# Converting float64 weights in word operations: carrying the sign through ScalarE's scaling instead of a second VectorE operation

## The chip, the cores and the metric

The kernel runs on one NeuronCore of one Trainium2 chip. The metric is the time of one execution on the device, in microseconds (us). The time of before is the median of three runs.

## The reference

The inputs are float64; the output is float32 of 4352 x 512. Three layers follow each other: an attention between x (8 batches, 8 heads, 512 rows, width 64) and a state of 32 rows per batch and head, and two gated layers.

```python
scores = scale * np.matmul(x, state.transpose(0, 1, 3, 2))      # softmax, then xread = a @ state
scores2 = scale * np.matmul(state, x.transpose(0, 1, 3, 2))     # softmax, then sread = a2 @ x
x = np.concatenate([xread, sread], axis=2)                      # reshaped to 4352 x 512
x = (x @ w1) * (x @ w2) @ w3 @ w_out                            # moe: 512 -> 1024 -> 512
x = (x @ w_a) * (x @ w_b) @ w_out                               # moe2: 512 -> 1536 -> 512
```

What matters here is that all seven weight matrices arrive as float64 and must be made float32 on the chip before TensorE can use them.

## The kernel before, in words

**Tiles and buffers.** SBUF is handed out as 47 numbered units of 128 x 1024 words, PSUM as 8 banks of 128 x 512. A unit that is taken again carries the wait for its former use with it, on whatever engine writes it first, a load's queue included.

**The conversion.** A load brings 128 x 512 float64 numbers (512 KB) into one unit as pairs of 32-bit words. Such a load is called a piece. `Convert` (from L154) makes float32 of a piece in four operations:

- `take` (L165): two ScalarE activations. The first (L167) reads the upper words as float32 and multiplies them by 2^-112, in place. Seen as a float32, the upper word of a float64 has the upper 8 of the 11 exponent bits as its exponent, so the scaling subtracts 112 there, which is 896 = 1023 - 127 in the exponent of the float64. The second (L170) scales the lower words by 2^-29 into integers.
- `shift` (L172): a VectorE `tensor_scalar` (L176) moves the upper words left by 3 bits; exponent and mantissa are then where float32 has them, and the sign is shifted out. A VectorE `scalar_tensor_tensor` (L179) takes the sign bit of the unshifted word by a bitwise and, and puts it into the result by a bitwise or.
- `add` (L183): a GpSimd integer addition (L185) puts in the bits of the lower word, and the unit of the load becomes free.

There are 92 pieces: 40 at the start (20 names of two pieces in `EARLY`, L24), 16 for the first gated layer's state path (`sw`), and 36 for the second layer (`ab`: twelve column blocks of two pieces, each with one piece of the output matrix).

**Stages.** At the start, the pieces of `w_out` (`wo`) are converted and split into a high and a low float32r part (`woh` by ScalarE L297, `wol` by VectorE or GpSimd L303); those of `w3` are converted, transposed by TensorE (L347), split (`w3h`, `w3l`), and multiplied by `w_out` in `weight_product` (L361), which needs all of `wo`; `ws` is the result. The pieces of `w1` and `w2` (`wk`) are multiplied by the state (L318), copied to SBUF (`sg`, L330 and L332), stored to DRAM per batch (L336, `p_d`) on SP's queue, and loaded again (L593, `pr`), split into `ph` (L136) and `pl` (L142), and multiplied by the attention weights (`f`, L1054). In the middle, batch after batch goes through the first layer (L1054, L1113) while the attention of the next batch and the `sw` and `ab` conversions are laced in. From some 600 us on, the second layer runs (L1500, L1512), TensorE's long part; it uses no conversion after 700 us.

**What sets the order.** The program is written out by hand, one queue per engine. At the start, `run_jobs` (L646) is a list scheduler: each `Job` (L603) names its engine, a price in us, its predecessors and the units and banks that it needs; the job that can start first by these prices is written next. `convert_jobs` (L678) makes the jobs of a piece: ScalarE 1.3, VectorE 1.45 (L691), GpSimd 1.3. Jobs that may go to either of two engines (`wol`, `sg`) are put where they would end first by the prices. In the middle, `Intake` (L898) holds the steps of `sw` and `ab` blocks, each with its prices (`V=1.8, G=2.4` for two pieces, L997; `V=0.9, G=1.2` for one, L1008); a step is written once the time counted for its engines has come near. These prices are numbers in the program that orders the instructions; the chip doesn't see them.

Of the kernel before, what the change touches and what calls it, by code (L numbers as in the profile page):

```python
# [9 lines left out]
F32 = mybir.dt.float32  # L10
# [4 lines left out]
AF = mybir.ActivationFunctionType  # L15
ALU = mybir.AluOpType
# [43 lines left out]
def attention_moe_moe2(  # L60
# [17 lines left out]
    nc = tc.nc  # L78
# [38 lines left out]
    def unit(name, dt=F32):  # L117
        assert name not in held, name
        first = min(range(len(vacant)), key=lambda i: vacant[i][0])
        held[name] = vacant.pop(first)[1]  # L120
        return up.tile([P, 1024], dt, tag=f"u{held[name]}", name=name)

    def free(*names, at=None):
        for name in names:
            vacant.append((at or until[0] or now[0], held.pop(name)))
# [23 lines left out]
    def load64(name, src):  # L149
        t = unit(name, U32)  # L150
        nc.sync.dma_start(out=t if len(src.shape) == 2 else flat(t, src.shape[2]), in_=src)
        return name, t

    class Convert:  # L154
# [10 lines left out]
        def take(self, i):  # L165
            c, d = self.words(i)
            nc.scalar.activation(  # L167
                out=c.bitcast(F32), in_=c.bitcast(F32), func=AF.Copy, scale=2.0**-112
            )
            nc.scalar.activation(out=d.bitcast(I32), in_=d, func=AF.Copy, scale=2.0**-29)  # L170

        def shift(self, i):  # L172
            if self.out is None:
                self.out = unit(self.name)[:, : self.n]
            c, out = self.words(i)[0], self.out[:, i * 512 : (i + 1) * 512].bitcast(U32)
            nc.vector.tensor_scalar(  # L176
                out=out, in0=c, scalar1=3, scalar2=None, op0=ALU.logical_shift_left
            )
            nc.vector.scalar_tensor_tensor(  # L179
                out=out, in0=c, scalar=0x80000000, in1=out, op0=ALU.bitwise_and, op1=ALU.bitwise_or  # L180
            )

        def add(self, i):  # L183
# [487 lines left out]
    def load_job(time, go, need, lag=1.0):  # L671
        j = Job("D", time, go, behind=loads[-1:], need=need, keep=KEEP if len(loads) < KEEP_UNTIL else 1, prio=len(loads), lag=lag)
        loads.append(j)
        return j

    conv = {}

    def convert_jobs(name):  # L678

        adds = []  # L680
        conv[name] = Convert(name, [None, None])
        for i, v in enumerate(parts[name]):

            def load(i=i, v=v):
                conv[name].raws[i] = load64(f"{name}r{i}", v)

            l = load_job(1.7, load, 1)
            if len(loads) == 1:
                state_jobs()
            t = Job("A", 1.3, lambda i=i: conv[name].take(i), after=[l], prio=2)  # L690
            s = Job("V", 1.45, lambda i=i: conv[name].shift(i), after=[t] + adds, need=1 - i, prio=2)  # L691
            adds = adds + [Job("G", 1.3, lambda i=i: conv[name].add(i), after=[s], prio=2)]
        return adds

# [121 lines left out]
    for name in EARLY:  # L816
# [3 lines left out]
        elif name[:2] == "wo":  # L820
            i = int(name[2])
# [3 lines left out]
        elif name[:2] == "w3":  # L825
            i = int(name[3])
            adds = convert_jobs(name)
            lows, trs = [], []
            for k in range(2):
# [4 lines left out]
                    after=list(adds),  # L834
                    prio=0,
# [6 lines left out]
                    after=[tr] + lows,  # L842
                    need=2 - 2 * k,
                    prio=1,
# [6 lines left out]
                        after=[h],  # L851
                        prio=1,
# [20 lines left out]
        else:  # L873
            b = int(name[1])
            done = []
            for g in range(2):
                l = load_job(3.5, lambda b=b, g=g: load_x_half(b, g), 1, 2.0)
                t = Job("P", 1.8, lambda b=b, g=g: attn[b].x_transpose(g), after=[l], need=1, prio=1, banks=("ps", 2))
# [19 lines left out]
    class Intake:  # L898
# [27 lines left out]
        def stages(self, f, raws):  # L926

            o = {}
            name = f"{self.name}{f}"
            eng = "GV"[f % 2]  # L930

            def take(i):
                if i == 0:
                    o["c"] = Convert(name, raws[:2])
                o["c"].take(i)

            def take_third():
                o["t"] = Convert(f"{name}t", raws[2:])
                o["t"].take(0)

            def split_columns():
                hi, lo = unit(f"{name}h", F32R), unit(f"{name}l", F32R)
                split(hi, lo, o["c"].out, {"G": nc.gpsimd, "V": nc.vector}[eng])
                free(name)
                self.cols[f] = [v.rearrange("p (w k c) -> p w k c", k=4, w=2) for v in (hi, lo)]

            def halves(t):
                return t.rearrange("p (b c) -> p b c", b=4)

            def sums():  # L950
                a21, a22, a11, a12 = (halves(o["c"].out)[:, i] for i in range(4))
                o["s"] = unit(f"{name}s")
                s1, s2, s3, s4 = (halves(o["s"])[:, i] for i in range(4))
                e = {"G": nc.gpsimd, "V": nc.vector}[eng]
                for out, x, y, op in (
                    (s1, a21, a22, ALU.add),
                    (s3, a11, a21, ALU.subtract),
                    (s2, s1, a11, ALU.subtract),
                    (s4, a12, s2, ALU.subtract),
                ):  # L960
                    e.tensor_tensor(out=out, in0=x, in1=y, op=op)

            def split_part(i):
                src, part = ((o["c"].out, name), (o["s"], f"{name}s"))[i]
                hi, lo = (unit(f"w0_{f}_{2 * i + j}", F32R) for j in range(2))
                split(hi, lo, src, {"G": nc.gpsimd, "V": nc.vector}["VG"["GV".index(eng)]])
                free(part)
                o["p", i] = hi, lo

            def store_part(i):  # L970
                for j, t in enumerate(o["p", i]):
                    nc.sync.dma_start(out=w_d[f][:, 2 * i + j].bitcast(F32), in_=t.bitcast(F32))
                if f in AB_AT:
                    free(*(f"w0_{f}_{2 * i + j}" for j in range(2)), at=until[0] + 2.5)
                else:
                    w_t.setdefault((0, f), []).extend(
                        t.rearrange("p (b k c) -> p b k c", b=4, k=2) for t in o["p", i]
                    )
                self.cols[f] = i == 1

            def split_third():
                z = o["z"] = flat(unit(f"z{f}", F32R), DM)
                split(z[:, 0, :], z[:, 1, :], o["t"].out)
                free(f"{name}t")

            def store_third():
                nc.sync.dma_start(out=z_d[f].bitcast(F32), in_=o["z"].bitcast(F32))
                if f in AB_AT:
                    free(f"z{f}", at=until[0] + 2.5)
                else:  # L990
                    z_t[f] = o["z"]
                self.rows[f] = True

            out = [
                (0, dict(A=1.1), lambda: take(0)),
                (0, dict(A=1.1), lambda: take(1)),
                (1, dict(V=1.8, G=2.4), lambda: o["c"].make()),  # L997
            ]
            if self.third is None:
                out.append((2, {"A": 1.1, eng: {"G": 2.4, "V": 1.1}[eng]}, split_columns))  # L1000
            else:
                other = "VG"["GV".index(eng)]
                work = {"A": 1.1, other: {"G": 2.4, "V": 1.1}[other]}
                out += [
                    (0, dict(A=1.1), take_third),
                    (1, {eng: {"G": 2.6, "V": 1.4}[eng]}, sums),
                    (2, work, lambda: split_part(0)),
                    (1, dict(V=0.9, G=1.2), lambda: o["t"].make()),  # L1008
                    (0, dict(D=3.0), lambda: store_part(0)),
                    (2, work, lambda: split_part(1)),  # L1010
                    (1, dict(A=0.6, V=0.6), split_third),
                    (0, dict(D=3.0), lambda: store_part(1)),
                    (0, dict(D=1.5), store_third),
                ]
            return deque(out)
# [301 lines left out]
    for b, qs in ((0, range(4)), (1, range(3))):  # L1317
        for q in qs:
# [4 lines left out]
                after=stores[q // 2] + ([last] if last else []),  # L1323
                need=1,
                prio=1 + 20 * b,
# [7 lines left out]
    for f in range(NF1):  # L1333
# [4 lines left out]
            after=[ready[0, f // 2], attended[0][0]],  # L1338
# [12 lines left out]
    for p in range(NP):  # L1351
        for nh in range(2):
            products = []
            moves = {0: [], 1: []}
            for i in range(2):
# [4 lines left out]
                    after=[last],  # L1360
                    need=2 - 2 * i,
                    keep=LATE_KEEP,
                    prio=LATE_PRIO,
# [10 lines left out]
            for r in range(2):  # L1374
# [4 lines left out]
                    after=moves[r],  # L1379
                    prio=len(loads) + STORE_BEHIND,  # L1380
# [4 lines left out]
    for j in range(4):  # L1385
        o = Job("P", 5.5, lambda j=j: first_output(j), after=lows + w_done + moves[-2:-1], prio=8, banks=("ps", 1))
# [399 lines left out]
```

## Time and profile before

| what | us |
|---|---|
| median of the three runs | 1377.65 |
| lowest and highest of them | 1375.01, 1380.78 |
| span of the profiled execution (first to last instruction) | 1376.4 |
| TensorE (PE) busy | 1308.8 |
| VectorE (DVE) busy | 697.6 |
| ScalarE (ACT) busy | 550.8 |
| GpSimd (POOL) busy | 445.2 |

The profiled execution's own time is recorded only as its span; what lies around the span is taken as the 1.25 us by which the median is longer. In the profile, PE is TensorE's matmuls, PEld its weight loads; a name with a q behind it is that engine's queue. A window row gives, for each engine, busy us and, in brackets, the number of instructions, then the granted TensorE clock as a share of full speed, the DMA share and GB/s. A row of waits gives who waited for whom, the total, the times, and the longest.

### The profile page before, as it was taken

To read this page: it belongs to the slowest core of one execution; us is meant where nothing else is said; L and a number is where in the kernel's file an instruction comes from. 1 tells how busy PE (TensorE), PEld (TensorE's weight loads), DVE (VectorE), ACT (ScalarE), POOL (GpSimd) and SP (SyncE) were. 2 spreads that over 40 slices of the span, in tenths; PEclk is the share of its full clock that TensorE was granted. 3 is DMA by queue.
4 is the path that set the end of the run, shared out by engine and by line. 5 is a ranking of instruction groups with operands and counts; after the bars stand their busy time and mean duration, and the time that the engine had idled before them with its cause. 6 is when DMAs were issued, how large, how long until landed. Compare 5 with 4: busy or idle time off the path is not lost.

```text
span 1376.4 us, 17480 instructions
## 1 busy us (share of the span) xinstructions
PE 1308.8 (95%) x6596; PEld 1056.0 (77%) x6596; DVE 697.6 (51%) x879; ACT 550.8 (40%) x955; POOL 445.2 (32%) x353
## 2 busy tenths in 40 slices
PE   2888999999999998999999999999999999999998
PEld 1655678788777777988888888888888888888877
DVE  7997405666768767566652442232632224532241
ACT  6676534556555565454431322211412223311230
POOL 4543402554465465445530152111311112310010
PEclk6899999999999999999999999999999999999999
DMA  9675758364655651467554436443464443744401
GB/s 321 219 222 181 216 160 242 133 210 167 225 184 174 224 168 63 139 229 291 185 194 171 169 122 230 153 145 116 152 233 165 153 138 122 262 158 145 140 0 62
DMA packets 120661, 240.24 MB, mean 175 GB/s; under 512 B 44672, under 2 KB 65152, under 8 KB 120576
## 3 DMA queue, kind: packets, MB, share of 16 engines
q1 hardware_dynamic: 116000, 222.86, 48.8%
q0 software_dynamic: 4576, 16.26, 3.1%
q8 instruction: 52, 0.85, 0.2%
q14 instruction: 33, 0.27, 0.1%
HBM read 173.54 MB, written 65.54 MB: 174 GB/s over the span
## 4 chain that ended last, share of the span: by engine, by line
PE 70%; DVE 5%; ACT 2%; issue 2%; DMA 1%; POOL 1%; SPq 0%; DVEq 0%; POOLq 0%; ACTq 0%
PE o L1512 19%; PE r L1500 18%; PE v L1500 9%; PE x2p L1113 6%; PE q L1500 5%; PE bp L1054 3%; PE ap L1054 3%; PE abs L1555 2%; PE os L1584 1%; DVE sw L179 1%; PE x2s L1113 1%; DMA w_d<-w 1%; DMA z<-z_d 1%; PE as L1054 1%; PE bs L1054 1%
## 5 line engine op out<-in xcount | busy, mean ns | idle before, releaser
L1512 PE MATMUL o<-z,h 128*128 128x512 f32 x1152 | 276.8, 389 | 2.1 <-ACT h L136 1.3
L1512 PEld LDWEIGHTS o<-z,h 128*128 128x128 f32 x1152 | 216.0, 188 | 48.2 <-ACT h L136 1.7
L1675 POOL TENSOR_TENSOR hb<-e,e 128x512 f32<-128x512 f32 x48 | 62.8, 1309 | 448.5 <-DVE e L1525 448.5
L136 ACT CAST h<-e 128x512 fp32r<-128x512 f32 x48 | 29.8, 620 | 369.7 <-DVE e L1678 355.6
L1113 PE MATMUL x2p<-hp,ws 128*128 128x512 f32 x672 | 161.9, 390 | 0.0
L1113 PEld LDWEIGHTS x2p<-hp,ws 128*128 128x128 f32 x672 | 125.7, 188 | 26.3
L1525 DVE TENSOR_TENSOR e<-e,q 128x512 f32<-128x512 f32 x48 | 33.0, 687 | 193.9 <-PE q L1500 193.9
L142 POOL TENSOR_TENSOR pl<-pr,ph 128x512 fp32r<-128x512 f32 x64 | 85.6, 1357 | 114.7 <-ACT ph L136 99.5
L1078 DVE TENSOR_TENSOR hfp<-asbp,bp 128x512 f32<-128x512 f32 x56 | 38.2, 682 | 77.7 <-PE bp L1054 76.0
L1525 DVE TENSOR_TENSOR e<-e,v 128x512 f32<-128x512 f32 x48 | 32.9, 686 | 80.4 <-PE v L1500 80.4
L1500 PE MATMUL r<-xT4h,w 128*128 128x512 f32 x192 | 67.3, 391 | 2.6 <-DVE e L1525 2.6
L136 ACT CAST hp<-hfp 128x512 fp32r<-128x512 f32 x56 | 34.7, 619 | 81.4 <-DVE hfp L1078 78.9
L142 DVE TENSOR_TENSOR hp<-hfp,hp 128x512 fp32r<-128x512 f32 x56 | 46.8, 836 | 40.0 <-ACT hp L136 38.6
L1500 PE MATMUL r<-xT2h,w 128*128 128x512 f32 x192 | 67.1, 390 | 0.0
L1500 PE MATMUL r<-xB11h,w 128*128 128x512 f32 x192 | 66.9, 389 | 0.0
L1500 PE MATMUL v<-xT1h,w 128*128 128x512 f32 x192 | 66.9, 389 | 0.0
L1500 PE MATMUL q<-xB21h,w 128*128 128x512 f32 x192 | 66.9, 389 | 0.0
L1500 PE MATMUL r<-xT3h,w 128*128 128x512 f32 x192 | 66.9, 389 | 0.0
L1500 PE MATMUL v<-xB22h,w 128*128 128x512 f32 x192 | 66.9, 389 | 0.0
L1054 PE MATMUL bp<-ah,ph 128*128 128x512 f32 x112 | 48.7, 435 | 5.0 <-DVE hfs L1078 3.1
L142 DVE TENSOR_TENSOR h<-e,h 128x512 fp32r<-128x512 f32 x48 | 35.1, 732 | 33.4 <-ACT h L136 33.4
L1072 ACT COPY asbp<-ap 128x512 f32<-128x512 f32 x56 | 32.8, 585 | 46.2 <-PE ap L1054 46.1
(505 smaller groups left out, 2928.1 us busy)
## 6 DMA issues: line engine op xcount, KB each, us to landing
w<-w_d SPq DMA_DIRECT2D x168, 512.0 KB, 5.2
w_d<-w SPq DMA_DIRECT2D x48, 512.0 KB, 2.7
p_d<-sg SPq DMA_DIRECT2D x128, 128.0 KB, 2.5
pr<-p_d SPq DMA_DIRECT2D x32, 512.0 KB, 5.4
x<-in_x_dram SPq DMA_DIRECT2D x64, 128.0 KB, 3.7
sw<-in_moe_w_dram SPq DMA_DIRECT2D x16, 512.0 KB, 5.1
xB<-x_d SPq DMA_DIRECT2D x16, 512.0 KB, 5.1
x_d<-x2sp POOLq DMA_DIRECT2D x14, 512.0 KB, 5.7
```

The source lines that it names most:

```text
L136: nc.scalar.copy(hi, src)
L142: (eng or nc.vector).tensor_tensor(out=lo[:, i], in0=src[:, i], in1=hi[:, i].bitcast(F32), op=ALU.subtract)
L179: nc.vector.scalar_tensor_tensor(out=out, in0=c, scalar=0x80000000, in1=out, op0=ALU.bitwise_and, op1=ALU.bitwise_or)
L1054: nc.tensor.matmul(dst[:, :n], lhsT=l[m], rhs=r[q], start=i == 0 and j == 0, stop=i == k - 1 and j == 2,)
L1072: nc.scalar.copy(a_sb[:, :n], pa[:, :n])
L1078: nc.vector.tensor_tensor(out=hf[:, :n], in0=a_sb[:, :n], in1=pb[:, :n], op=ALU.mult)
L1113: nc.tensor.matmul(acc[j], lhsT=w_s[f][:, m, j * P : (j + 1) * P], rhs=h[:, q, :n], start=per == 1 and f == 0 and i == 0, stop=f == NF1 - ...
L1500: nc.tensor.matmul(t, lhsT=w[m], rhs=xf[g].parts[x][q][:, k, :], start=first and k == 0 and i == 0, stop=k == 1 and i == 2, skip_group_che ...
L1512: nc.tensor.matmul(t, lhsT=h[:, m, part * P : (part + 1) * P], rhs=z_t[f][:, q, :], start=first and c == 0, stop=last and c == 2,)
L1525: nc.vector.tensor_tensor(out=out, in0=x, in1=y, op=ALU.add)
L1555: nc.tensor.matmul(t[:, w * 256 : (w + 1) * 256], lhsT=l[m], rhs=x_s[k][q], start=k == 0 and i == 0, stop=k == 3 and i == 2,)
L1675: nc.gpsimd.tensor_tensor(out=h2[-1][:, f % 2, :], in0=e2, in1=e5, op=ALU.mult)
```

## The change

The sign no longer passes through VectorE. ScalarE's first activation becomes a Prelu: positive numbers are scaled as before, negative ones also by the slope 2^32. That adds 32 to the exponent field of a negative word, whose field is below 32 after the scaling, so it sets the field's bit 5, and the shift left by 3 puts that bit where float32 has its sign. The `scalar_tensor_tensor` is removed. Three prices of the order are changed with it.

```diff
@@ take
             nc.scalar.activation(
-                out=c.bitcast(F32), in_=c.bitcast(F32), func=AF.Copy, scale=2.0**-112
+                out=c.bitcast(F32), in_=c.bitcast(F32), func=AF.Prelu, scale=2.0**-112, alpha=2.0**32
             )
@@ shift
             nc.vector.tensor_scalar(
                 out=out, in0=c, scalar1=3, scalar2=None, op0=ALU.logical_shift_left
-            )
-            nc.vector.scalar_tensor_tensor(
-                out=out, in0=c, scalar=0x80000000, in1=out, op0=ALU.bitwise_and, op1=ALU.bitwise_or
             )
@@ convert_jobs
-            s = Job("V", 1.45, lambda i=i: conv[name].shift(i), after=[t] + adds, need=1 - i, prio=2)
+            s = Job("V", 0.75, lambda i=i: conv[name].shift(i), after=[t] + adds, need=1 - i, prio=2)
@@ Intake.stages
-                (1, dict(V=1.8, G=2.4), lambda: o["c"].make()),
+                (1, dict(V=1.2, G=2.4), lambda: o["c"].make()),
@@
-                    (1, dict(V=0.9, G=1.2), lambda: o["t"].make()),
+                    (1, dict(V=0.6, G=1.2), lambda: o["t"].make()),
```

## Rows read from the trace of the kernel before

**Rows 1.** The page: busy time and share by engine, then PE in 40 equal slices.

```profile
PE 1308.8 (95%) x6596; PEld 1056.0 (77%) x6596; DVE 697.6 (51%) x879; ACT 550.8 (40%) x955; POOL 445.2 (32%) x353
...
PE   2888999999999998999999999999999999999998
```

**Rows 2.** Busy time of each engine in five stretches of the span.

```profile
10.00:40.00 30.00, 4.62 (x17) 3.38 (x18) 29.42 (x34) 22.60 (x42) 18.27 (x13) 0.50 1.05 353
40.00:130.00 90.00, 82.26 (x466) 56.76 (x465) 84.27 (x105) 63.41 (x123) 41.03 (x30) 0.99 0.67 204
130.00:200.00 70.00, 63.80 (x258) 42.43 (x256) 18.09 (x21) 32.33 (x58) 17.69 (x14) 0.95 0.60 178
200.00:760.00 560.00, 542.11 (x3141) 446.37 (x3142) 349.14 (x441) 281.31 (x490) 261.37 (x206) 0.99 0.56 187
760.00:1376.40 616.40, 610.36 (x2701) 504.63 (x2700) 215.24 (x276) 146.95 (x239) 104.86 (x84) 1.00 0.43 149
```

**Rows 3.** PE in order of time (start, us, what): the first weight product.

```profile
39.48 0.78 PE L361 MATMUL wp<-woh,w3h 128*128 128x512 f32 x1
```

**Rows 4.** DVE in order of time, three places of the start.

```profile
39.13 0.68 DVE L303 TENSOR_TENSOR wol<-wo,woh 128x512 fp32r<-128x512 f32 x1
...
43.75 0.69 DVE L179 SCALAR_TENSOR_TENSOR w<-w_0r,w 128x512 uint32<-128x512 uint32 x1
44.36 0.68 DVE L303 TENSOR_TENSOR w3l<-w3t,w3h 128x512 fp32r<-128x512 f32 x1
...
89.65 1.52 DVE L176 TENSOR_SCALAR wk<-wk_1r 128x512 uint32<-128x512 uint32 x1
91.20 1.66 DVE L179 SCALAR_TENSOR_TENSOR wk<-wk_1r,wk 128x512 uint32<-128x512 uint32 x1
```

**Rows 5.** Line 179 alone in three stretches: us, DVE busy, clock, DMA.

```profile
10.00:40.00 30.00, 15.07 (x12) 0.50 1.05 353
40.00:130.00 90.00, 28.52 (x27) 0.99 0.67 204
...
200.00:760.00 560.00, 63.89 (x52) 0.99 0.56 187
```

**Rows 6.** POOL in order of time, an addition beside the last rows of DVE.

```profile
90.83 1.47 POOL L185 TENSOR_TENSOR w<-w,w_6r 128x512 int32<-128x512 int32 x1
```

**Rows 7.** ACT, lines 167, 433: forms with duration ns min/median/max, first and last start.

```profile
L167 ACT ACTIVATE ab<-ab x24: 639/678/697, 229.6 to 696.4; 128x512 f32<-128x512 f32 x24
...
L167 ACT ACT_TABLE_LOAD  x1: 1283/1283/1283, 0.7 to 0.7; - x1
...
L433 ACT ACTIVATE e<-s,nm x16: 708/713/728, 70.0 to 474.3; 128x512 f32<-128x512 f32 x16
```

**Rows 8.** What the last wo pieces need: their issue on SP, landing, ACT's waits.

```profile
8.80 1.03 SPq L151 DMA_DIRECT2D wo2r<-in_moe_w_out_dram  x2
...
wo2r<-in_moe_w_out_dram SPq DMA_DIRECT2D x2, 512.0 KB, 10.0
...
ACT woh L297 <- POOL wo L185: 5.9, 5, 1.8
```

**Rows 9.** PE's waits from 40 to 200 us, and SP's queue near their end.

```profile
PE f L1054 <- ACT ph L136: 4.4, 2, 3.4
PE w3t L347 <- DVE w3l L303: 2.5, 1, 2.5
...
PE pb L318 <- POOL wk L185: 1.6, 1, 1.6
...
106.06 22.02 SPq L336 DMA_DIRECT2D p_d<-sg  x24
128.18 0.39 SPq L593 DMA_DIRECT2D pr<-p_d  x1
```

**Rows 10.** 480 to 570 us: all engines; then PE's longest wait for DVE there.

```profile
480.00:570.00 90.00, 82.75 (x491) 70.41 (x490) 62.30 (x74) 50.88 (x82) 54.74 (x39) 0.96 0.35 116
...
548.24 0.79 PE L1054 MATMUL bp<-ah,ph 128*128 128x512 f32 x1 [3.05 <-DVE hfs L1078]
```

## The prediction

> **What bounds the kernel now.** I read the page first: TensorE is busy for 1308.8 of 1376.4 us, and its slices show where the rest is, at the start and a little in the middle [rows 1]. The windows by stage give it: from 10 to 40 us PE is busy for 4.62 us while DVE is busy for 29.42 of 30; from 40 to 130 us DVE is still at 84.27 of 90, and PE idles 90 - 82.26 = 7.7; from 130 to 200 PE idles 6.2, from 200 to 760 17.9, after that 6.0 in 616 us [rows 2]. So the start is bound by VectorE, the rest by TensorE, with small gaps in the middle. Nothing that the change touches runs after 760 us. What can be had lies in the 25.4, 7.7, 6.2 and 17.9 us of idle PE.
>
> The order of DVE at the start shows why PE waits: the last `wol` starts at 39.13 us, and the first weight product at 39.48 [rows 3, 4]. Since 10 us DVE had no gap to speak of, so every operation ahead of that `wol` sets the moment at which PE begins.
>
> **The price of the operation removed.** Line 179 takes 15.07 us for 12 between 10 and 40 us, 28.52 for 27 up to 130, 63.89 for 52 from 200 to 760 [rows 5]. That is two things. By itself one takes 0.69 us, and the next starts 0.61 after it [rows 4], so bare the three stretches hold 7.3, 16.5 and 31.7 us. The rest, 15.07 - 12 x 0.69 = 6.8 us, then 9.9 and 28.0, is waiting: the one at 91.20 took 1.66 us and ended 0.56 us behind the addition that GpSimd ended at 92.30 [rows 4, 6]. The shift at 89.65 was held up too, 1.52 us [rows 4]. Whether this waiting goes with the operation or moves to the shift behind it isn't in the trace; I take the bare 0.61 as sure, and the waiting as the upper bound.
>
> The Trainium skill says under "SBUF — State Buffer" (the section with the diagram of the ports) that VectorE and GpSimd share a port pair as an exclusive lock, held for a whole instruction, by VectorE in a 2-port mode or with two SBUF inputs. By that rule alone all the waiting would move to the shifts, and the first term below would be the bare 7.3 and not the 14.1 with the waiting; the slow shift agrees with it.
>
> **What is added.** A Prelu for a Copy in line 167, median 0.678 us [rows 7]. The trace has no Prelu. The nearest row is another function on the same shape, the exponential with 0.713 [rows 7]; so 0 to 0.04 us a piece, 0.5 for the 12 pieces ahead of the first product. I take 0. A second activation table is a rival below.
>
> **Term 1, the start of PE.** With the bare price `wol` comes 12 x 0.61 = 7.3 us earlier, with all waiting 14.1. What is late next is ScalarE: it is busy for 22.60 of 30 us [rows 2], and its waits for GpSimd's additions ahead of `woh`, which are what a faster VectorE shortens, are 5.9 us in all [rows 8]; more comes only if the new order puts fewer `take` ahead of the last `woh`. The loads are no floor: `wo2` was issued up to 9.83 us and landed 10.0 later [rows 8], near 20 us. GpSimd has 18.27 of 30 [rows 2]. Between 4 (most of ScalarE's waits stay) and 12 (a better order as well) I take **7**, where the bare price and ScalarE's waits nearly meet. PE was at 0.50 of its clock, 1.2 GHz, before 40 us and at 0.99 from there [rows 2]; a ramp comes in any case, only earlier.
>
> **Term 2, 40 to 130 us.** DVE is relieved by 16.5 us and is no longer the bound; PE's 82.26 is. Its 7.7 us of idle time are short waits on VectorE and GpSimd, `w3l` with 2.5 and the `wk` additions with 1.6 among them [rows 9]. I take **4**, bounds 0 and 7.7.
>
> **130 to 200 us.** Here the wait is for `ph`, 4.4 us: it needs a reload of `p_d` that stands in SP's queue behind 24 stores, 22.02 us [rows 9]. Those stores wait for `sg`, which comes from TensorE's products, so they move with PE, and I count 0, with 3 us on either side for the re-ordered queue.
>
> **Term 3, 200 to 760 us.** DVE is at 349.14 of 560 [rows 2], so most of the 31.7 bare us lie beside PE's work. PE idles where a chain through DVE is late: 7.25 of 90 us from 480 to 570, the longest wait 3.05 for `hfs` of DVE [rows 10]. I take **4** of the 17.9, bounds 0 and 10.
>
> **Moved.** Three prices change the written order: jobs that can go to two engines are drawn to VectorE more, `Intake` steps come earlier. The old shift price of 1.45 stood against bare 0.69 and some 0.4 plus waits; the new one leaves one operation of about 0.41 to 1.52 at 0.75. I see no bias, count 0, and give it a rival. No DMA is added or taken away.
>
> **Sum.** 7 + 4 + 4 = 15 us from the profiled 1376.4, so 1361.4; with the 1.25 us around the span that makes **1362.7**, 1.1% below the median of 1377.65. All lower ends together give 1376, all upper ends (12 + 7.7 + 3 + 10 = 32.7) 1345. A measurement of this kernel can tell about 0.5%, 6.9 us.
>
> **Rivals.**
> *It is given back at the reload.* PE starts earlier but arrives at the wait for `ph` earlier too, because SP's stores and the DRAM round trip set the restart at 135 us. For it: 22 us of SP's queue [rows 9]. Against: the stores' own sources come earlier. Terms 1 and 2 go, term 3 stays: 1373.7.
>
> *Activation tables change (the slower side).* The trace has one table load of 1.283 us, at 0.7 us, for Copy, Identity and Exp together [rows 7]. If Prelu isn't in that set, each group of exponentials among the conversions costs two loads. There are 8 batches with two groups each (16 instructions of line 433 in pairs, from 70 to 474 us [rows 7], and a row exponential a batch), so up to 32 loads or 41 us of ScalarE, with nothing to hide them at the start and about half hidden in the middle, where ScalarE is at 281.31 of 560 [rows 2]. With two thirds on the path, 27 - 15 = 12 us slower: 1390. It decides from 15 / 1.283, or 12 loads on PE's path, on. For it: nothing in the trace shows Prelu. Against: three functions share a set already. The Trainium skill, "ScalarE: Activation LUTs", section on table sets, names relu, copy, identity and abs as filler of every set, not Prelu, and about 2.66 us for a switch; by that figure 32 switches would be some 85 us, an estimate; in this trace the load is 1.283.
>
> *The new order is worse.* Two store groups of 8 are written ahead of the reload, 2 x 22.02 x 8 / 24 = 14.7 us [rows 9], and eat all three terms: 1377.3, no change; a third would make it slower.
>
> [...]
>
> **How the numbers follow.** The forecast 0.68 (nearly all of it faster by over 0.5%, 0.02 within), given back at the reload 0.14 (0.04 faster, 0.10 within), tables 0.10 (0.08 slower, 0.02 within), worse order 0.08 (0.05 within, 0.03 slower). Faster 0.70, same 0.19, slower 0.11. The range runs from 1347, nearly all upper ends, to 1381, beyond the cases of no change; it leaves out the tables' case and a little on the fast side.
>
> **What would show it.** Line 179 is gone; line 167 stays near 0.68; the table load stays x1. The first L361 starts near 32 us instead of 39.48. DVE falls from 29.42 of 30 in the first stretch, and by 92 x 0.61 = 56 us or more in all. The shifts' mean shows whether the waiting moved to them. PE's idle time from 40 to 130 and from 200 to 760 falls by 4 each. Wrong if there are more table loads, if L361 starts early and the wait for `ph` grows by as much, or if DVE stays full because the additions now hold up the shifts.

## The result, and the profile after

The changed kernel takes 1342.45 us (median) against 1378.24 for the one before in the same comparison: a ratio of 0.9738, with an interval from 0.972 to 0.9755, or 35.8 us less. The forecast was 1362.7 with a range of 1347 to 1381: the direction was right, the size was not, and the time lies below the range. One of the changed kernel's four executions took 2818.22 us, more than twice the others (1341.06 to 1342.51), for a reason that isn't known, and doesn't enter the ratio.

The page of the changed kernel, busy time by engine and PE in 40 slices, against [rows 1]:

```profile
PE 1300.3 (97%) x6596; PEld 1054.2 (79%) x6596; DVE 612.0 (46%) x792; ACT 550.2 (41%) x951; POOL 439.3 (33%) x352
...
PE   3998999999999999999999999999999999999998
```

VectorE does 85.6 us less and ScalarE the same. The dark slices of PE in the middle are gone as well as some of the start. The first weight product starts at 32.70 us, against 39.48 in [rows 3]; line 167 has its old duration as a Prelu, and there is still one table load, against [rows 7]. All lines behind `shift` have numbers lower by 3 than before. First PE in order of time, then the forms of line 167:

```profile
32.70 0.77 PE L358 MATMUL wp<-woh,w3h 128*128 128x512 f32 x1
```

```profile
L167 ACT ACTIVATE ab<-ab x24: 642/670/697, 212.7 to 660.8; 128x512 f32<-128x512 f32 x24
...
L167 ACT ACT_TABLE_LOAD  x1: 1283/1283/1283, 0.7 to 0.7; - x1
```

Windows at fixed times compare different work once one kernel runs ahead. So the span is cut where PE begins something: the first weight product (`wp`), the first `f`, the first batch's `ap`, the first `as` of the state path, the first `r` of the second layer, and the first `os`. From `ap` on the two kernels do the same PE work in each stretch. Before (us of the stretch, then busy us and instructions of PE, PEld, DVE, ACT, POOL, granted clock, DMA share, GB/s):

```profile
0.00:39.50 39.50, 9.76 (x35) 5.30 (x35) 30.32 (x37) 26.64 (x46) 19.75 (x20) 0.60 1.00 318
39.50:135.00 95.50, 84.32 (x475) 57.78 (x473) 87.47 (x108) 64.64 (x125) 41.53 (x30) 0.98 0.67 204
135.00:199.90 64.90, 62.14 (x249) 41.77 (x249) 15.39 (x18) 31.14 (x57) 17.69 (x14) 0.95 0.60 177
199.90:515.20 315.30, 306.00 (x1869) 242.87 (x1868) 211.39 (x257) 180.71 (x319) 158.52 (x129) 1.00 0.59 193
515.20:593.00 77.80, 72.74 (x435) 64.66 (x434) 49.80 (x62) 37.59 (x62) 39.55 (x27) 0.96 0.39 128
593.00:814.60 221.60, 218.08 (x1094) 184.62 (x1093) 117.91 (x155) 83.59 (x139) 85.69 (x67) 1.00 0.52 188
814.60:1376.40 561.80, 555.76 (x2449) 458.94 (x2448) 185.28 (x245) 126.46 (x209) 82.47 (x69) 1.00 0.43 150
```

The changed kernel, cut at the same places:

```profile
0.00:32.70 32.70, 9.68 (x34) 5.10 (x35) 19.91 (x26) 25.07 (x45) 19.01 (x19) 0.63 0.98 312
32.70:117.10 84.40, 81.25 (x458) 56.24 (x456) 58.08 (x78) 60.09 (x114) 39.25 (x30) 0.98 0.87 264
117.10:183.00 65.90, 62.48 (x266) 43.23 (x266) 18.34 (x23) 34.30 (x65) 17.24 (x14) 0.97 0.45 139
183.00:492.00 309.00, 305.32 (x1869) 243.02 (x1868) 187.29 (x233) 183.43 (x323) 157.05 (x130) 1.00 0.63 203
492.00:561.10 69.10, 69.10 (x435) 62.53 (x435) 41.49 (x51) 37.35 (x61) 40.83 (x27) 1.00 0.44 143
561.10:778.20 217.10, 216.87 (x1094) 184.95 (x1093) 101.55 (x138) 83.44 (x138) 83.39 (x67) 1.00 0.54 193
778.20:1340.70 562.50, 555.64 (x2449) 459.08 (x2447) 185.35 (x245) 126.56 (x209) 82.48 (x69) 1.00 0.44 150
```

The stretches got shorter by 6.8, 11.1, -1.0, 6.3, 8.7, 4.5 and -0.7 us. That is 16.9 us up to the first batch and 19.5 in the middle. Of the 19.5, PE's idle time makes 14.0 (9.3 + 5.1 + 3.5 before, 3.7 + 0 + 0.2 after), and PE's own busy time for the same instructions 5.5, most of it (72.74 to 69.10) in the state path's stretch, where the granted clock was 0.96 before.

### The profile page after: what moved, and what is told of

Same layout as the page of the kernel before. It is cut to its first block, busy times and chain, and to the rows that moved or that the text cites. A ratio compares the mean times of both kernels' runs of the same rounds, so it can differ in the third digit from the quotient of the medians.

```text
span 1340.7 us, 17395 instructions
## 1 busy us (share of the span) xinstructions
PE 1300.3 (97%) x6596; PEld 1054.2 (79%) x6596; DVE 612.0 (46%) x792; ACT 550.2 (41%) x951; POOL 439.3 (33%) x352
## 4 chain that ended last, share of the span: by engine, by line
PE 89%; DMA 4%; DVE 3%; ACT 2%; issue 1%; POOL 1%; SPq 1%; ACTq 0%; POOLq 0%; DVEq 0%
PE r L1497 20%; PE o L1509 19%; PE v L1497 10%; PE x2p L1110 9%; PE bp L1051 5%; PE q L1497 5%; PE ap L1051 5%; PE abs L1552 3%; PE wp L358 2%; PE pb L315 2%; PE x2f L1291 2%; PE f L1051 1%; PE os L1581 1%; PE xt L388 1%; PE bs L1051 1%
## 5 line engine op out<-in xcount | busy, mean ns | idle before, releaser
L142 DVE TENSOR_TENSOR hp<-hfp,hp 128x512 fp32r<-128x512 f32 x56 | 54.1, 965 | 40.0 <-ACT hp L136 38.7
L1069 ACT COPY asbp<-ap 128x512 f32<-128x512 f32 x56 | 33.1, 591 | 56.3 <-PE ap L1051 56.2
```

The source lines that it names most:

```text
L142: (eng or nc.vector).tensor_tensor(out=lo[:, i], in0=src[:, i], in1=hi[:, i].bitcast(F32), op=ALU.subtract)
L1069: nc.scalar.copy(a_sb[:, :n], pa[:, :n])
```

## The experiments

### The operations or the order

Two kernels take the change apart. One has its operations with the old prices, so that every queue is written as before but for line 179; the other has the new prices with the old operations. The first is the change without its last three hunks, the second has these alone:

```diff
-            s = Job("V", 1.45, lambda i=i: conv[name].shift(i), after=[t] + adds, need=1 - i, prio=2)
+            s = Job("V", 0.75, lambda i=i: conv[name].shift(i), after=[t] + adds, need=1 - i, prio=2)
...
-                (1, dict(V=1.8, G=2.4), lambda: o["c"].make()),
+                (1, dict(V=1.2, G=2.4), lambda: o["c"].make()),
...
-                    (1, dict(V=0.9, G=1.2), lambda: o["t"].make()),
+                    (1, dict(V=0.6, G=1.2), lambda: o["t"].make()),
```

> The change's operations with the old prices: the order of every queue is that of before, only line 179 is missing on VectorE. If the operation alone carries the gain (theory A), 1342 to 1350. If the re-planned order carries a good part of it (theory B), 1352 to 1365. First weight product near 33 us by both.

> The old operations with the new prices: the order of the changed kernel, with line 179 still in it. Theory A: 1372 to 1385, no gain without the operation gone. Theory B: 1355 to 1368.

Operations alone: 1347.11 us against 1378.73, ratio 0.9779 (0.9752 to 0.9806), 31.6 us. Prices alone: 1374.30, ratio 0.9969 (0.9959 to 0.9979), 4.4 us. The two add up to 36.0. So theory A holds: the operation carries the gain, and the order adds a little on its own. The kernel with the operations alone shows the same middle as the changed one; at the start it has the same first product, and less after it (its second, fourth and fifth stretch):

```profile
32.80:122.60 89.80, 84.37 (x475) 59.85 (x473) 54.53 (x80) 64.42 (x126) 38.89 (x30) 0.96 0.80 242
...
186.50:495.60 309.10, 305.43 (x1870) 243.00 (x1869) 188.37 (x233) 182.95 (x322) 157.05 (x130) 1.00 0.61 197
495.60:564.60 69.00, 69.00 (x435) 62.47 (x434) 41.45 (x51) 37.17 (x61) 40.67 (x27) 1.00 0.43 142
```

The first batch begins at 186.5 us there, 13.4 earlier than before; the order brings the other 3.5.

### Bare time or waiting

The removed operation was bare time and waiting for GpSimd [rows 5, 6]. Two kernels each put one of these back into the changed kernel. The first has a reduction over the same words ahead of the shift, the second the old operation on 16 of its 512 columns, where it changes nothing, as the sign is there already.

```diff
+            junk = sm.tile([P, 1], F32, tag="junk", name="junk")
+            nc.vector.tensor_reduce(out=junk, in_=c.bitcast(F32), axis=AX.X, op=ALU.max)
             nc.vector.tensor_scalar(
                 out=out, in0=c, scalar1=3, scalar2=None, op0=ALU.logical_shift_left
             )
```

```diff
             nc.vector.tensor_scalar(
                 out=out, in0=c, scalar1=3, scalar2=None, op0=ALU.logical_shift_left
             )
+            nc.vector.scalar_tensor_tensor(
+                out=out[:, :16], in0=c[:, :16], scalar=0x80000000, in1=out[:, :16], op0=ALU.bitwise_and, op1=ALU.bitwise_or
+            )
```

> The changed kernel with a VectorE reduction over the same 512 words ahead of each shift: it has about the bare time of the removed operation (0.6 us) but one SBUF input, so it should not wait for GpSimd. If the gain is mostly waiting that went (theory C), 1342 to 1352. If it is mostly bare time (theory D), 1360 to 1378, and the first weight product is back near 39 us.

> The changed kernel with the removed operation on 16 of its 512 columns: nearly no bare time (0.1 us), but it can wait for GpSimd as the old one did. Theory C: 1360 to 1378, its mean far over 0.1 us by 0.5 us or so. Theory D: 1342 to 1350.

The reduction: 1355.39 us, 12.9 above the changed kernel's 1342.45. The 16 columns: 1349.39, 6.9 above it. Both theories expected one of the two to bring back nearly all. The reduction lies between what C and D said of it; the 16 columns lie just inside what D said. The first weight product, which D had back near 39 us with the reduction, starts at 35.1 (33.5 with the 16 columns, 32.7 without either). So neither theory holds as a whole. The forms of the two added operations (duration ns min/median/max) show that each was what it was meant to be. The reduction, with one input in SBUF, never waits:

```profile
L177 DVE TENSOR_REDUCE junk<-ab x24: 645/678/689, 223.8 to 678.1; 128x1 f32<-128x512 f32 x24
L177 DVE TENSOR_REDUCE junk<-sw x16: 639/676/687, 444.3 to 542.4; 128x1 f32<-128x512 f32 x16
```

The 16 columns take 0.176 us where nothing stands in the way, and up to 2.0 us:

```profile
L179 DVE SCALAR_TENSOR_TENSOR ab<-ab,ab x24: 174/662/1549, 221.4 to 670.9; 128x16 uint32<-128x16 uint32 x24
L179 DVE SCALAR_TENSOR_TENSOR sw<-sw,sw x16: 174/1152/2014, 441.6 to 537.3; 128x16 uint32<-128x16 uint32 x16
```

What stands in the way is GpSimd. Of the 92, 39 took longer than 0.3 us, and each of these ran beside a GpSimd instruction; most ended 0.02 to 0.05 us behind the end of one, as the first of them did. DVE and POOL in order of time:

```profile
15.25 1.15 DVE L179 SCALAR_TENSOR_TENSOR wo<-wo0r,wo 128x16 uint32<-128x16 uint32 x1
```

```profile
15.01 1.36 POOL L185 TENSOR_TENSOR wo<-wo,wo3r 128x512 int32<-128x512 int32 x1 [1.23 <-DVE wo L179]
```

All 92 of them are busy for 56.2 us, of which 92 x 0.176 = 16.2 are bare and 40.0 waiting, nearly the 44.7 of before (108.2 us of line 179 in all, less 92 x 0.69). The kernel with the new prices and the whole old operation has the same order as these two, and lies 31.9 us above the changed one: bare time and waiting together cost more than the 12.9 + 6.9 that each costs alone. From `ap` to `os` they do add up: 595.2 us in the changed kernel, 605.9 with the reduction, 601.1 with the 16 columns, 612.8 with the whole operation (10.7 + 5.9 against 17.6). Up to `ap` they don't: 183.0, 187.2, 184.5 and 195.8 (4.2 + 1.5 against 12.8). There VectorE has room now (22.09 of 30 us busy from 10 to 40) and is full with both (29.45); that the first few us fall into this room is how I read it, not a thing that a run shows by itself.

### The start or the middle

The operations of the change for the pieces of the start alone, and for those of the middle alone, with the old prices, so in the order of before:

```diff
-            self.name = name
+            self.name, self.new = name, name[0] == "w"
...
-                out=c.bitcast(F32), in_=c.bitcast(F32), func=AF.Copy, scale=2.0**-112
+                out=c.bitcast(F32), in_=c.bitcast(F32), scale=2.0**-112, **(dict(func=AF.Prelu, alpha=2.0**32) if self.new else dict(func=AF.Copy))
...
+            if not self.new:
                 nc.vector.scalar_tensor_tensor(out=out, in0=c, scalar=0x80000000, in1=out, op0=ALU.bitwise_and, op1=ALU.bitwise_or)
```

For the middle the condition is `name[0] != "w"`.

> The change's operations for the 40 pieces of the start alone (wo, w3, wk), old prices, order of before. If the terms of the prediction had the right proportion (theory E: start 11, middle 4), nearly all the gain is here: 1350 to 1358 by the 31.6 us of the run with all operations. If the middle was the mis-sized term (theory F), 1363 to 1367: the start gives 13 us and the middle keeps its full length of 614.7 us from the first ap to the first os.

> The change's operations for the 52 pieces of the middle alone (sw, ab), old prices, order of before. Theory E: 1372 to 1376. Theory F: 1358 to 1362, first ap near 200 us as before, and 595 us from there to the first os; the stretch of half clock near 547 us is gone.

The start alone: 1364.89 us against 1376.58, ratio 0.9908 (0.9892 to 0.9925), 11.7 us. The middle alone: 1358.18, ratio 0.9865 (0.985 to 0.988), 18.4 us. That is theory F: the proportion of the prediction was wrong, and the middle was the term that it had too small. Together they make 30.1 of the 31.6.

### Which part of the middle

The same with the condition `name[:2] == "sw"` (16 pieces) and `name[:2] == "ab"` (36 pieces):

> The change's operations for the 16 sw pieces alone, old prices, order of before. Line 179 takes 21.6 us there. If the gain follows the share of VectorE's time (theory G: 18.4 us for 63.9), 6 us: 1370 to 1372. If the sw stage loses more because there the conversion's burst stands between PE's results and its next operands, and a PE wait brings half clock behind it (theory H), 8 to 12 us: 1365 to 1369, with 69 to 70 us from the first as to the first r instead of 77.8 and no half clock near 547 us.

> The change's operations for the 36 ab pieces alone, old prices, order of before; line 179 takes 42.3 us there. Theory G: 12 us, 1363 to 1366. Theory H: 6 to 10 us, 1367 to 1371, the sw stage from the first as to the first r still 75 to 78 us, and the 221.6 us from the first r to the first os down to 217 to 218.

`sw` alone: 1368.04 us against 1378.08, ratio 0.9926 (0.9911 to 0.9941), 10.0 us. `ab` alone: 1369.28, ratio 0.9937 (0.9914 to 0.9959), 8.8 us. The 16 pieces give about as much as the 36 (10.0 and 8.8 don't differ beyond their intervals), where theory G had 6 and 12; so the gain doesn't follow VectorE's time (21.6 and 42.3 us of line 179) but where the pieces stand: theory H. The stretches from `as` to `r` and from `r` to `os` show it. With `sw` alone:

```profile
514.80:583.80 69.00, 69.00 (x435) 62.49 (x434) 43.47 (x52) 36.88 (x60) 39.97 (x27) 1.00 0.44 143
583.80:805.30 221.50, 218.14 (x1094) 184.67 (x1093) 118.09 (x155) 83.76 (x139) 85.73 (x67) 1.00 0.53 189
```

With `ab` alone:

```profile
511.10:588.90 77.80, 72.76 (x435) 64.73 (x434) 47.72 (x61) 38.00 (x63) 40.27 (x27) 0.96 0.38 125
588.90:806.00 217.10, 216.88 (x1094) 184.96 (x1093) 98.71 (x138) 83.34 (x138) 82.91 (x67) 1.00 0.54 193
```

The first of these stretches falls from 77.8 to 69.0 us by the `sw` pieces alone and not at all by the `ab` pieces; the second the other way round, 221.6 to 217.1. The stretch ahead of them, from `ap` to `as`, falls by both: from 315.3 us to 313.4 with `sw` alone, 311.0 with `ab` alone, 309.0 with both.

PE's longest waits in the middle before (from 183 to 815 us; who waited for whom, the total, the times, the longest) go the same way:

```profile
PE srt L520 <- ACT sn L513: 4.3, 3, 2.2
PE bp L1054 <- DVE hfs L1078: 3.1, 1, 3.1
PE r L1500 <- DVE e L1525: 2.6, 3, 1.7
```

With `sw` alone the wait for `hfs` is gone and those for `e` are as before; with `ab` alone it is the other way round. The waits for `sn` fall to 2.4 us with `sw` alone and to 2.2 with `ab` alone. In the changed kernel 0.2 us is left of the three.

The place in the trace of the longest wait is a burst of two pieces on VectorE. Before, all engines but PEld from 543.5 us, without what doesn't touch it:

```profile
543.51 0.42 DVE L176 TENSOR_SCALAR sw<-sw 128x512 uint32<-128x512 uint32 x1
...
543.97 0.69 DVE L179 SCALAR_TENSOR_TENSOR sw<-sw,sw 128x512 uint32<-128x512 uint32 x1
...
544.58 0.42 DVE L176 TENSOR_SCALAR sw<-sw 128x512 uint32<-128x512 uint32 x1
...
544.89 1.28 POOL L185 TENSOR_TENSOR sw<-sw,sw 128x512 int32<-128x512 int32 x1 [4.73 <-DVE sw L179]
...
545.03 1.69 DVE L179 SCALAR_TENSOR_TENSOR sw<-sw,sw 128x512 uint32<-128x512 uint32 x1
...
546.64 1.21 DVE L142 TENSOR_TENSOR xT1l<-xB,xT1h 128x1024 fp32r<-128x1024 f32 x1
...
547.78 0.41 DVE L1078 TENSOR_TENSOR hfs<-asbs,bs 128x256 f32<-128x256 f32 x1
```

After, DVE at the same piece of the program:

```profile
516.23 0.76 DVE L176 TENSOR_SCALAR sw<-sw 128x512 uint32<-128x512 uint32 x2
...
516.89 1.22 DVE L142 TENSOR_TENSOR xT1l<-xB,xT1h 128x1024 fp32r<-128x1024 f32 x1
...
518.03 0.42 DVE L1075 TENSOR_TENSOR hfs<-asbs,bs 128x256 f32<-128x256 f32 x1
```

The two pieces held VectorE's queue for 3.13 us (543.51 to 546.64), and now for 0.66. `hfs` stands behind them, and `hfs` is what PE waited for, for 3.05 us [rows 10]; after, PE has no idle time in the whole stretch. The longest wait for `e` has the same form: before, two `ab` pieces hold VectorE's queue from 652.07 to 655.17 us, `e` stands behind them, and PE waits. DVE, then PE, in order of time:

```profile
652.07 0.41 DVE L176 TENSOR_SCALAR ab<-ab 128x512 uint32<-128x512 uint32 x1
...
655.17 0.67 DVE L1525 TENSOR_TENSOR e<-e,r 128x512 f32<-128x512 f32 x1
```

```profile
655.90 0.50 PE L1500 MATMUL r<-xT4h,w 128*128 128x512 f32 x1 [1.69 <-DVE e L1525]
```

What holds up `sn` is not traced here.

In the trace of before, the wait for `hfs` also had a tail. The granted clock fell during it, to 0.50 or 1.2 GHz from 547.2 to 554.0 us; and the twelve `x2s` products, which took 2.76 us there, take 1.60 in the changed kernel. The stretch of half clock and the group before:

```profile
547.20:554.00 6.80, 5.76 (x21) 5.18 (x22) 3.65 (x6) 3.43 (x5) 6.80 (x4) 0.50 0.00 0
```

```profile
550.97 2.76 PE L1113 MATMUL x2s<-hs,ws 128*128 128x256 f32 x12
```

and after:

```profile
520.38 1.60 PE L1110 MATMUL x2s<-hs,ws 128*128 128x256 f32 x12
```

With `sw` alone there is no such stretch of half clock in the middle; with `ab` alone it is there, 6.8 us long, as before. But the tail doesn't follow every such wait. The kernel with the prices alone still has the old operations, and PE waits for `hfs` just as long; yet the granted clock stays at 1.00 there, and the twelve products take 1.60 us:

```profile
544.12 0.50 PE L1054 MATMUL bp<-ah,ph 128*128 128x512 f32 x1 [3.05 <-DVE hfs L1078]
...
545.62 1.60 PE L1113 MATMUL x2s<-hs,ws 128*128 128x256 f32 x12
```

Its stretch from `as` to `r` is 76.0 us long, with 70.44 us of PE busy. So of the 8.7 us that this stretch got shorter, the half clock can be given some 2, and the waits themselves the larger part.

### A version that goes further

With the sign in place, shift and addition can be one operation, if ScalarE's second scaling gives the lower three bits truncated. GpSimd's addition of each piece goes:

```diff
-            nc.scalar.activation(out=d.bitcast(I32), in_=d, func=AF.Copy, scale=2.0**-29)
+            nc.scalar.activation(out=d.bitcast(I32), in_=d, func=AF.Copy, scale=2.0**-29, bias=-0.5)
...
-            nc.vector.tensor_scalar(
-                out=out, in0=c, scalar1=3, scalar2=None, op0=ALU.logical_shift_left
+            d = self.words(i)[1]
+            nc.vector.scalar_tensor_tensor(
+                out=out, in0=c, scalar=3, in1=d, op0=ALU.logical_shift_left, op1=ALU.bitwise_or
             )
...
-            nc.gpsimd.tensor_tensor(out=out, in0=out, in1=d.bitcast(I32), op=ALU.add)
```

> The changed kernel, with ScalarE's second scaling shifted by -0.5 so that it gives the lower three bits truncated, and shift and or of them in one VectorE operation; GpSimd's addition of each piece is gone (the last bit of a weight is truncated instead of rounded). Prices as in the changed kernel. If the remaining idle time of the start hangs on GpSimd's additions, 1332 to 1340; if ScalarE or the loads bound it by now, 1341 to 1345; slower if VectorE's longer operation (0.69 for 0.42) is back on the path, 1346 to 1352.

> The same with the prices of the order set to it: nothing for GpSimd, 1.4 and 0.7 for VectorE. 2 to 6 us below the run with the old prices if the order follows the shorter chain, else within 2 of it.

> Shift and or in one VectorE operation without GpSimd's addition, with the price of 0.02 for GpSimd at the start, and the middle's prices of the changed kernel. The run with new prices in both places began its batches 3.5 us earlier than the one with the changed kernel's prices and lost 6.5 in all, behind the first r. If the loss came from the middle's prices, 1333 to 1336; if the start's order brought it, 1342 to 1345.

With the changed kernel's prices: 1337.81 us, ratio to before 0.9719 (0.9704 to 0.9733), inside the range for idle time that hangs on GpSimd's additions. With prices set to the new chain in both places: 1344.35, 0.9765 (0.975 to 0.9779), so worse by 6.5, which neither reading had, though its first product starts at 22.3 us and its first batch at 175.1. With the new price at the start alone: 1335.11, 0.969 (0.9674 to 0.9707), as expected: the middle's prices had brought the loss. The last is the fastest of the study, 7.3 us below the changed kernel. At the start VectorE's new operation hardly meets GpSimd any more and takes 0.69 us (DVE in order of time):

```profile
15.40 0.69 DVE L177 SCALAR_TENSOR_TENSOR wo<-wo0r 128x512 uint32<-128x512 uint32 x1 [0.33 <-ACT wo0r L170]
16.01 0.68 DVE L303 TENSOR_TENSOR wol<-wo,woh 128x512 fp32r<-128x512 f32 x1
17.02 0.69 DVE L177 SCALAR_TENSOR_TENSOR wo<-wo0r 128x512 uint32<-128x512 uint32 x1 [0.33 <-ACT wo0r L170]
```

Its first product starts 9.7 us earlier than the changed kernel's (23.0 against 32.7), but its first batch only 4.9 earlier (178.1 against 183.0): 6.9 us are given back in the stretch from `wp` to `f`, 91.3 us against 84.4, and 2.1 won again in the next, 63.8 against 65.9.

## Why the prediction was right or wrong

**What bounds the kernel.** Right for the start; DVE was at 29.42 of 30 us there and is at 22.09 now. In the middle the bound was named rightly, but the "small gaps", 17.9 us of idle time, were taken too lightly: all but some 4 of them went with VectorE's operation.

**Term 1, 7 us.** Right: 6.8 us (39.5 to 32.7), and 6.7 with the operations alone. ScalarE's waits for GpSimd ahead of `woh` went from 5.9 [rows 8] to 1.5 us, as the step had it. That "a ramp comes in any case" does not hold for every execution: in the one profiled with the prices alone the granted clock was 1.00 from 10 to 40 us, with PE busy for 4.67 us of them, where before had 0.50 with 4.62.

**Term 2, 4 us, and 0 from 130 to 200.** Near: in the order of before the stretch from `wp` to `f` got shorter by 5.7 us (95.5 to 89.8) and the next by 1.0. The reload did not give it back: `f` starts 12.4 us earlier with the operations alone and 17.9 in the changed kernel. That rival falls.

**Moved, 0 us.** Here 3.5 us too little up to the first batch, 4.4 in all by the run with the prices alone. The rival of a worse order falls; the fused kernels show that prices alone can move a kernel by 6.5 us and more.

**Term 3, 4 us.** This is the step that failed: "most of the 31.7 bare us lie beside PE's work", with an upper bound of 10. The runs show 18.4 us (middle alone), by the stretches 19.5. I had divided VectorE's load by the length of the stage, 349.14 of 560, and taken the rest as room. But the pieces come two at a time, and what counts is what stands behind each pair in the queue: 3.13 us ahead of `hfs`, where the mean load says nothing. The bound should have been the whole idle time of PE, 17.9, plus what PE's busy time could lose, which I took as nothing: it fell by another 5.5 us, 3.6 of them in the stretch with that wait. By the kernel with the prices alone (70.44 us busy there, without the half clock, against 72.74) the half clock behind the wait makes about 2.3 of these. What made the remaining 3.2 us I don't know.

**The price of the operation.** Bare time sure, waiting as the upper bound: both parts cost time, 12.9 and 6.9 us put back alone. Of the waiting, about a third moved to other operations. With the operations alone, in the old order, VectorE's total falls by 697.6 - 603.4 = 94.2 us, where line 179 held 108.2; so, on balance, 14.0 of the 44.7 us of waiting came back at other operations. It did not go to the shifts, 59.7 us before and 58.0 there. The Trainium skill ("SBUF — State Buffer", section "SBUF: two separate sides") puts under the lock any VectorE operation with two SBUF inputs beside a GpSimd operation that reads SBUF. The trace agrees at two such operations: with the operations alone the mean of `wol` is 1.148 us, against 0.755 before, and that of `hp` (line 142) 0.939 against 0.836. That all the waiting would move to the shifts does not follow from the rule, and was my reading.

**Tables.** The rival falls: one load, as before, and 0.670 us median for the Prelu against 0.678 for the Copy. The exponential and Prelu share a set in this kernel.

**The range.** Its lower end was nearly the sum of all upper ends; with 18 in place of 10 for the middle, that sum would have held the result. All lower ends together come to 1376.7 us, not 1376.

## What to carry to other kernels

An engine that is busy for 60% of a stage can still hold up the one that bounds it. Find the bursts in its queue, and price an operation by what stands right behind it where the bounding engine waits; its upper end is at least all the idle time of the bounding engine in the stage. A wait of TensorE can cost again, as work at 1.2 GHz behind it, but here it did so in some executions and not in others. And cut two traces at the same piece of work, not at the same time, before comparing them.

## What the runs showed of the hardware

A ScalarE Prelu with a slope of 2^32 and a scale of 2^-112 runs at 0.670 us on 128 x 512, as the Copy, without a second table load. A VectorE operation with two SBUF inputs on 16 columns takes 0.176 us alone and up to 2.01 us beside GpSimd, so a small size did not spare it the wait; a reduction with one SBUF input on 512 columns stayed between 0.639 and 0.689 us through the same stretches. And a wait of PE of 3.05 us ended, in the trace of before, in a stretch of 6.8 us at a granted clock of 0.50, in which twelve products took 2.76 instead of 1.60 us; the same wait in the kernel with the prices alone was followed by none.
